# Top-k attention with two expert layers: all rests of the gate and value weights on GpSimd, and plain float32 scores on 64 array rows each

## The chip, the core and the metric

The kernel runs on one core of a Trainium2 chip. The engines named below are TensorE (PE: matrix products, with its weight loads shown apart as PEld), VectorE (DVE), ScalarE (ACT), GpSimd (POOL), and SyncE (SP), whose queue issues nearly all the transfers (DMA). The metric is the device time of one execution in microseconds (us). Three runs of the kernel before gave 1229.64, 1230.01 and 1234.19 us, so the median is 1230.01 us.

## The reference

Three stages in a row, all in float32:

```
scores = (q @ k.T) / sqrt(64)            # 4 batches, 8 heads, 576 tokens, head size 64
keep the 32 largest scores of each row, softmax over them, attn @ v
x   = heads side by side                  # 2304 tokens x 512
x   = (silu(x @ w_gate) * (x @ w_val)) @ w_out      # 512 -> 1536 -> 512
h   = x @ w_in;  out = (h * cos(h)) @ w_out2        # 512 -> 2048 -> 512
```

Which 32 scores are kept must agree with the reference, so the scores need nearly full float32 precision.

## The kernel before, in words

**The stages.** The 18 tiles of 128 tokens are handled in ten chunks of 1, 1, 2, 2, ... tiles. A unit is one tile and one head: there are 144 of them. For each unit PE computes a 128 x 576 score tile into the two PSUM banks of `sc`, ACT copies it to SBUF (L679), DVE finds the 32 largest values with four MAX8 and three MATCH_REPLACE8 (L706, L709), POOL makes two bounds of them (L720, L724), ACT masks and exponentiates (L737, L748), PE turns the result (L770) and multiplies it by V (L823, L826). When the four head pairs of a chunk are done, its tokens go through the gate and value product (L1072 for the first two chunks, L981 for the others) and the output product of the first expert layer (L1146). The second expert layer follows from about 760 us on.

**Two ways to multiply.** A plain float32 product goes through PE as two passes per matmul in the trace (64 score matmuls of L661 are 128 records). From the third chunk on, the gate and value weights are used as a pair instead: a rounded part (type fp32r, one pass) and a rest, the float32 weight minus its rounded part. `w1_rest` makes the pair for each of 24 half blocks of weights, number `i`: ACT makes the rounded part (`hi`, L295), then a subtraction makes the rest (L299), on VectorE for odd `i` and on GpSimd for even `i`. A pair is written over the slot of the raw half block before it, so number `i` waits for number `i - 1`. All of this has to be there before the gate and value product of the third chunk.

**Plain scores.** The first three chunks (32 units) and the 64 query rows of tile 4 that lie in batch 0 (`edge_score`, for all 8 heads) use plain float32 scores. Both heads of a pair lie in one K tile `KR[p]`, head 0 on partitions 0 to 63 and head 1 on 64 to 127, 576 columns wide. The queries of one head fill 64 partitions and the other 64 are set to zero (memsets of L454 and L537), so each matmul runs over all 128 array rows with 288 columns and the other head adds nothing.

**What sets the order.** The program is written by a planner (`Plan`): every step is a generator that yields an engine, an estimated cost, a function and a due time. The planner keeps a clock for each engine and always takes the ready step with the earliest due time. So a changed cost or engine reorders the instructions of the whole program. At run time every engine works through its own list strictly in that order. Rings (`Ring`) gate the use of buffers: five score tiles, one PSUM score tile, two buffers for output weights (`wo`), one for raw K or Q (`raw`). Because SP is also a list in order, a transfer that waits for a buffer holds back those written behind it.

**The output weights.** `wo0_proc` converts 12 blocks (ACT, then POOL at L249) while the first chunk uses them and stores them; the second chunk loads each of them again (L376, "wo<-wo"), two buffers at a time.

Of the kernel before, what the change touches and what calls it, by code (L numbers as in the profile page):

```python
# [9 lines left out]
F32 = mybir.dt.float32  # L10
# [11 lines left out]
B, H, S, D = 4, 8, 576, 64  # L22
# [8 lines left out]
CH = 256  # L31
# [5 lines left out]
FIRST = [sum(SIZES[:c]) for c in range(NCH)]  # L37
# [11 lines left out]
HALF = S // 2  # L49
# [7 lines left out]
RAWC = 3  # L57
SC_LEAD = 14.0
# [107 lines left out]
def topk_attention_moe_moe(ctx: ExitStack, tc: tile.TileContext, qT, kT, vP, w1, wo1, w2, out):  # L166
    nc = tc.nc
# [27 lines left out]
    att = opened("att", side="right")  # L195
# [5 lines left out]
    sc = psR.tile([128, 2, 512], F32, name="sc")  # L201
# [75 lines left out]
    def w1_rest(i, raw, due):  # L277
        f, a = divmod(i, 2)
        t = yield from convert(raw, due, r_top[i % 2], i // 2, tops[i % 2], True)
        x = raw.bitcast(F32)[:, :DM]  # L280
        W1X[f, a] = x.rearrange("p (g k f) -> p g k f", g=2, k=2)
        r_pre.free(i, t, plan)
        if i == 2 * NF1 - 1:
            r_k.free(0, t, plan)
        ev_w1x[f].set(t, plan)
        yield ev_gemm[PLAIN - 1, f]
        if i:
            yield ev_w1s[i - 1]
        due = W1S_FIRST + W1S_STEP * i
        st = {}  # L290

        def hi():
            st["w"] = w = wpool.tile([128, 2, DM], F32R, tag=slot(i), name=f"w1_{f}")
            W1[f, a] = w.rearrange("p s (g k f) -> p s g k f", g=2, k=2)
            nc.scalar.activation(w[:, 0], x, AF.Copy)  # L295

        yield "ACT", 0.52, hi, due, True
        eng, name, cost = (nc.vector, "DVE", 0.75) if i % 2 else (nc.gpsimd, "POOL", 1.25)
        t = yield name, cost, lambda: eng.tensor_sub(st["w"][:, 1], x, st["w"][:, 0]), due, True  # L299
        ev_w1s[i].set(t, plan)  # L300
        ev_w1[f].set(t, plan)
# [93 lines left out]
    K, Q, V = {}, {}, {}  # L395
# [18 lines left out]
    r_k, r_v = Ring(NK), Ring(NV)  # L414
# [16 lines left out]
    KR, QR = {}, {}  # L431
# [10 lines left out]
    EDGE = S % 128  # L442
    TE = S // 128
# [4 lines left out]
    edge = {}  # L448

    def edge_proc():  # L450

        def clear():
            edge["q"] = att.tile([128, NP, 2, EDGE], F32, tag="K", name="qe", bufs=r_k.n)
            nc.vector.memset(edge["q"], 0.0)  # L454

        yield "DVE", 0.5, clear, -1.0, True

        def load():
            for h in range(2):
                rows = slice(64 * h, 64 * h + 64)  # L460
                nc.sync.dma_start(edge["q"][rows, :, h],
                                  qT[:, rows, TE * 128:TE * 128 + EDGE].rearrange("p d n -> d p n"))

        t = yield "DMA", 1.0, load, 2.0, True
        for p in range(NP):
            for h in range(2):
                plan.start(edge_score(p, h), t)

    def edge_score(p, h):
        n = 2 * p + h  # L470
        due = EDGE_DUE + n
        yield ev_kr[p]
        yield r_edge[h].gate(p)
        ps = gvt if h == 0 else yt

        def qk():
            for s in range(2):
                nc.tensor.matmul(ps[s][64 * h:64 * h + EDGE, :HALF], edge["q"][:, p, h],
                                 KR[p][:, s * HALF:s * HALF + HALF])

        t = yield "PE", 1.25, qk, due, True
# [30 lines left out]
    def k_raw_proc(p):  # L512

        def load():
            KR[p] = att.tile([128, S], F32, tag="K", name="kr", bufs=r_k.n)
            for h in range(0 if p else 2):
                nc.sync.dma_start(KR[p][64 * h:64 * h + 64], kT[0, p, 64 * h:64 * h + 64])
            if p:
                nc.sync.dma_start(KR[p], kT[0, p])

        t = yield "DMA", 1.3, load, due_unit(2 * p) - 40.0, True
        ev_kr[p].set(t, plan)

    def q_raw_proc(c, p):
        n = SIZES[c] * 128
        yield r_q.gate(q_index(c, p))

        def load():
            QR[c, p] = att.tile([128, 2, CH], F32, tag="q", name="qr", bufs=r_q.n)[:, :, :n]
            queue = nc.scalar if c == 0 and p == 0 else nc.sync  # L530
            for h in range(2):
                rows = slice(64 * h, 64 * h + 64)
                queue.dma_start(QR[c, p][rows, h], qT[p, rows, FIRST[c] * 128:FIRST[c] * 128 + n])

        def clear():
            for h in range(2):
                (nc.vector if c == 0 and p == 0 else nc.gpsimd).memset(QR[c, p][64 - 64 * h:128 - 64 * h, h], 0.0)  # L537

        due = due_unit(unit_of[c, p, 0, 0]) - 30.0
        if c == 0 and p == 0:  # L540
            load()
            clear()
            t = 3.2
        else:
            t = yield "DMA", 1.3, load, due, True
            t = yield "POOL", 0.5 if n == CH else 0.3, clear, due, True
        ev_qr[c, p].set(t, plan)

    def k_proc(i, b, p, h):
# [89 lines left out]
    def unit_proc(u):  # L639
        c, p, t, h = units[u]  # L640
        segs = segments(FIRST[c] + t)
        due = due_unit(u)
# [14 lines left out]

        def qk():
            if c < RAWC:
                for s in range(2):  # L660
                    nc.tensor.matmul(sc[:, s, :HALF], QR[c, p][:, h, t * 128:t * 128 + 128],  # L661
                                     KR[p][:, s * HALF:s * HALF + HALF])
                return
            for b, r0, r1 in segs[::-1]:
                if not b:
                    continue
                k = K[b, p, h]
                for s in range(2):
# [10 lines left out]
                nc.scalar.activation(st["s"], sc[:, :, :HALF], AF.Copy)  # L679

        yield r_sc.gate(u)
        end = yield "PE", 0.575 * len(cuts) if c >= RAWC else 0.98, qk, due - SC_LEAD, True
# [1176 lines left out]
```

## Time and profile before

| | |
|---|---|
| median of three runs | 1230.01 us |
| the profiled execution, its own time | 1227.0 us |
| span of its trace | 1225.1 us |
| PE busy in the span | 1174.1 us (96%), 7720 matmul records |
| DVE busy | 1001.4 us (82%) |
| ACT busy | 937.6 us (77%) |
| POOL busy | 564.1 us (46%), all of it before 800 us |
| chain that ended last | PE 66%, DVE 8%, ACT 8%, DMA 8%, POOL 5% of the span |

The profiled execution is 3.0 us faster than the median and 1.9 us longer than its span. A share of busy time is an average over stages with different limits: DVE is close to full until about 760 us, POOL has nothing to do after 800 us, and PE is close to full from 200 us to the end. So the stage in which an instruction lies decides what it is worth.

### The profile page before, as it was taken

What the parts mean: (1) busy time and instruction counts of PE and PEld (TensorE: products, weight loads), DVE (VectorE), ACT (ScalarE), POOL (GpSimd) and SP (SyncE); (2) the same over time, 40 slices, a digit from 0 to 9 for tenths busy, and PEclk for the clock granted to TensorE, in tenths of its full rate; (3) what the DMA queues carried; (4) which work ended last, traced back from release to release, by engine and by line L of the source; (5) the groups of instructions that cost most, each with busy time, mean ns of one, the idle gap of its engine ahead of it and who ended that gap; (6) DMA issues with size and microseconds to landing.
All of it is one profiled execution on the core that took longest, in us unless ns stands there. A gap on an engine that the chain in (4) does not pass through costs nothing.

```text
span 1225.1 us, 23258 instructions
## 1 busy us (share of the span) xinstructions
PE 1174.1 (96%) x7720; PEld 1018.1 (83%) x7720; DVE 1001.4 (82%) x1985; ACT 937.6 (77%) x2093; POOL 564.1 (46%) x1028
## 2 busy tenths in 40 slices
PE   6799978998999999999999999999999999999998
PEld 3477746897988898988988888889999998888886
DVE  7999999999999999998999997267877778644541
ACT  4979989988999889887898887345856678755651
POOL 4888875876787776876776765300000000000000
PEclk9899999999999999999999999999999999999999
DMA  8555457664556655666655533464344276443430
GB/s 261 181 180 160 142 152 223 202 213 154 181 177 193 200 185 175 185 180 186 193 175 166 165 98 104 152 201 132 134 158 143 104 249 202 146 120 104 129 104 26
DMA packets 139464, 200.08 MB, mean 163 GB/s; under 512 B 19792, under 2 KB 88912, under 8 KB 139344
## 3 DMA queue, kind: packets, MB, share of 16 engines
q1 hardware_dynamic: 139184, 198.54, 51.6%
q8 instruction: 61, 1.00, 0.3%
q14 instruction: 59, 0.48, 0.1%
q10 hardware_dynamic: 160, 0.07, 0.0%
HBM read 151.23 MB, written 47.32 MB: 162 GB/s over the span
## 4 chain that ended last, share of the span: by engine, by line
PE 66%; DVE 8%; ACT 8%; DMA 8%; POOL 5%; issue 3%; SPq 1%; POOLq 0%; ACTq 0%; DVEq 0%
PE b L1758 16%; PE b L1481 13%; PE gv L981 12%; PE y L1146 9%; DVE m L706 4%; DVE w L709 3%; PE tp L770 3%; PE av L826 3%; DMA wo<-wo 3%; PE sc L670 3%; PE gvl L981 2%; DMA y<-yo 2%; DMA qx<-in_qT 2%; PE gv L1072 1%; ACT e L748 1%
## 5 line engine op out<-in xcount | busy, mean ns | idle before, releaser
L706 DVE MAX8 m<-w 128x8 f32<-128x576 f32 x432 | 309.6, 748 | 1.6
L981 PE MATMUL gv<-x,w 128*128 128x256 f32 x2016 | 283.7, 288 | 1.6 <-ACT hg L948 1.6
L981 PEld LDWEIGHTS gv<-x,w 128*128 128x128 f32 x2016 | 258.5, 190 | 8.9 <-ACT hg L948 3.0
L709 DVE MATCH_REPLACE8 w<-m,w 128x576 f32<-128x576 f32 x288 | 213.0, 742 | 0.0
L1758 PE MATMUL b<-w2o,gp 128*128 128x512 f32 x864 | 202.1, 396 | 0.0
L1758 PEld LDWEIGHTS b<-w2o,gp 128*128 128x128 f32 x864 | 162.2, 188 | 39.0
L1481 PE MATMUL b<-xc,w 128*128 128x288 f32 x1344 | 182.1, 297 | 0.1
L1481 PEld LDWEIGHTS b<-xc,w 128*128 128x128 f32 x1344 | 180.0, 188 | 1.0 <-ACT s L1568 0.4
L1146 PE MATMUL y<-wo,gh 128*128 128x512 f32 x400 | 149.4, 415 | 7.1 <-DMA wo<-wo 4.9
L706 DVE MAX8 m<-s 128x8 f32<-128x576 f32 x144 | 107.3, 745 | 15.2 <-ACT s L679 12.9
L748 ACT ACTIVATE e<-e,b 128x576 f32<-128x576 f32 x144 | 114.9, 798 | 4.6 <-POOL b L724 1.7
L737 ACT ACTIVATE e<-s,b 128x576 f32<-128x576 f32 x144 | 114.4, 795 | 2.5 <-POOL b L720 2.3
L770 PE MATMUL tp<-ident,e 128*128 128x128 f32 x648 | 97.8, 274 | 9.5 <-ACT pt L776 7.5
L709 DVE MATCH_REPLACE8 w<-m,s 128x576 f32<-128x576 f32 x144 | 106.9, 742 | 0.0
L776 ACT ACTIVATE pt<-tp 128x512 f32<-128x512 f32 (+1 forms) x216 | 102.1, 507 | 5.5 <-PE tp L770 4.2
L679 ACT ACTIVATE s<-sc 128x576 f32<-128x576 f32 x136 | 91.0, 669 | 18.4 <-PE sc L661 15.5
L1146 PEld LDWEIGHTS y<-wo,gh 128*128 128x128 f32 x400 | 74.9, 189 | 29.3 <-issue 4.9
L770 PEld LDWEIGHTS tp<-ident,e 128*128 128x128 f32 x648 | 77.0, 140 | 20.7 <-ACT pt L776 12.0
L670 PE MATMUL sc<-K,q 128*128 128x288 f32 x480 | 86.0, 304 | 1.7 <-ACT s L679 1.1
L1146 PE MATMUL y<-wo,gl 128*128 128x512 f32 x208 | 84.7, 414 | 2.1 <-POOL wo L249 0.8
L1044 POOL TENSOR_TENSOR gl<-vv,gh 128x256 fp32r<-128x256 f32 x84 | 62.4, 743 | 38.5 <-ACT gh L1040 27.6
L826 PE MATMUL av<-pt,V 128*64 128x256 f32 (+3 forms) x832 | 75.1, 323 | 0.0
(123 smaller groups left out, 2100.8 us busy)
## 6 DMA issues: line engine op xcount, KB each, us to landing
wo<-wo SPq DMA_DIRECT2D x96, 512.0 KB, 3.8
gr<-gd SPq DMA_DIRECT2D x72, 256.0 KB, 3.2
w_raw<-in_w SPq DMA_DIRECT2D x32, 511.8 KB, 4.4
V<-in_vP SPq DMA_DIRECT2D x52, 256.0 KB, 3.1
w<-in_w SPq DMA_DIRECT2D x24, 511.5 KB, 6.1
wo<-wo SPq DMA_DIRECT2D x36, 256.0 KB, 3.0
gd<-h SPq DMA_DIRECT2D x32, 288.0 KB, 2.4
gd<-r SPq DMA_DIRECT2D x32, 288.0 KB, 2.2
```

Source lines behind the costliest of these rows:

```text
L670: nc.tensor.matmul(sc[:r1, s, :HALF], q[:, a, (t - t0) * 128:(t - t0) * 128 + r1], k[:, s * HALF:s * HALF + HALF], start=a == 0, stop=a == 1)
L706: nc.vector.max(out=st["m"][:, 8 * i:8 * i + 8], in_=st["w"] if i else st["s"])
L709: nc.vector.match_replace(out=st["w"], in_to_replace=st["m"][:, 8 * i:8 * i + 8], in_values=st["w"] if i else st["s"], imm_value=LOWEST)
L737: nc.scalar.activation(st["e"], st["s"], AF.Prelu, bias=st["b"][:, 1:2], scale=SCALE, alpha=STEEP)
L748: nc.scalar.activation(st["e"], st["e"], AF.Exp, bias=st["b"][:, 2:3], scale=1.0, accum_out=smT[c, p, g][:, j:j + 1])
L770: nc.tensor.transpose(st["ps"][:, j - j0], e[:, j * 128:j * 128 + 128], ident)
L776: nc.scalar.activation(pt[:, j0:j1], st["ps"][:, :j1 - j0], AF.Copy)
L826: nc.tensor.matmul(av[64 * h:64 * h + 64, r0:r1], m[:, j, h], pt[:, 5 * h + j, r0:r1], start=False, stop=j == 3)
L981: nc.tensor.matmul(gv[g], W1[f, kk // 2][:, a, g, kk % 2], m, start=kk == 0 and i == 0, stop=kk == KT - 1 and i == 2)
L1146: nc.tensor.matmul(bank, m, w, start=f == 0 and n == 0, stop=f == NF1 - 1 and n == len(terms) - 1)
L1481: nc.tensor.matmul(ps[b], w[:, a, side, kk], x[:, e, kk], start=start and kk == 0 and m == 0, stop=kk == 1 and m == 2, skip_group_check=True)
L1758: nc.tensor.matmul(st["o"], g[:, a, cs], W2O[f][:, b], start=f == 0 and i == 0, stop=f == NF2 - 1 and i == 2)
```

## The change

There are two edits, and the planner then writes the whole program anew.

First, the rests of all 24 half blocks are made by GpSimd. Second, the plain scores use 64 array rows each. The K tile now holds both heads on the same 64 partitions, the first 288 columns of both heads on partitions 0 to 63 and the last 288 columns on 64 to 127; the queries lie twice, once on each half. A score tile is then four matmuls of 144 columns in place of two of 288, alternating between the upper and lower 64 array rows, and the two halves write different PSUM banks. The zero halves of the queries, and with them the memsets, go. K is loaded in pieces of 288 columns in place of 576, with twice as many transfers, and the queries are read twice. The planner's costs for these steps change too, 0.98 to 0.8 for a unit and 1.25 to 0.8 for an edge score.

```
-        eng, name, cost = (nc.vector, "DVE", 0.75) if i % 2 else (nc.gpsimd, "POOL", 1.25)
+        eng, name, cost = nc.gpsimd, "POOL", 1.25
...
-            nc.vector.memset(edge["q"], 0.0)
...
         def qk():
-            for s in range(2):
-                nc.tensor.matmul(ps[s][64 * h:64 * h + EDGE, :HALF], edge["q"][:, p, h],
-                                 KR[p][:, s * HALF:s * HALF + HALF])
+            for j in range(0, HALF, HALF // 2):
+                for s in range(2):
+                    rows = slice(64 * s, 64 * s + 64)
+                    nc.tensor.matmul(ps[s][64 * h:64 * h + EDGE, j:j + HALF // 2], edge["q"][rows, p, h],
+                                     KR[p][rows, h, j:j + HALF // 2])
...
-            for h in range(0 if p else 2):
-                nc.sync.dma_start(KR[p][64 * h:64 * h + 64], kT[0, p, 64 * h:64 * h + 64])
-            if p:
-                nc.sync.dma_start(KR[p], kT[0, p])
+            for heads in (slice(0, 2),) if p else (slice(0, 1), slice(1, 2)):
+                for s in range(2):
+                    nc.sync.dma_start(KR[p][64 * s:64 * s + 64, heads], kT[0, p, :, s * HALF:s * HALF + HALF]
+                                      .rearrange("(h d) n -> d h n", h=2)[:, heads])
...
-        def clear():
-            for h in range(2):
-                (nc.vector if c == 0 and p == 0 else nc.gpsimd).memset(QR[c, p][64 - 64 * h:128 - 64 * h, h], 0.0)
...
             if c < RAWC:
-                for s in range(2):
-                    nc.tensor.matmul(sc[:, s, :HALF], QR[c, p][:, h, t * 128:t * 128 + 128],
-                                     KR[p][:, s * HALF:s * HALF + HALF])
+                for j in range(0, HALF, HALF // 2):
+                    for s in range(2):
+                        rows = slice(64 * s, 64 * s + 64)
+                        nc.tensor.matmul(sc[:, s, j:j + HALF // 2], QR[c, p][rows, h, t * 128:t * 128 + 128],
+                                         KR[p][rows, h, j:j + HALF // 2])
```

How the order moves is shown at two places. The first is POOL's list where the last rests are made, around the K and Q rests of the fourth chunk. In the names, `w_10_...` and `w_11_...` are half blocks of weight blocks 10 and 11 (the last number is a buffer's), `K<-kx` and `q<-qx` are the rests of K and Q, `rs` and `x` belong to the normalised attention output, `b` to the bounds. Before:

```order
L569 TENSOR_TENSOR K<-kx,K 64x576
L299 TENSOR_TENSOR w_10_1916<-w_10_818,w_10_1916 128x512
L896 TENSOR_TENSOR rs<-rx,rs 128x256
L720 TENSOR_TENSOR b_1944<-m,cst 128x2
L724 TENSOR_TENSOR b_1944<-b_1944 128x1
L907 TENSOR_TENSOR x<-rs,x 128x256
L596 TENSOR_TENSOR q<-qx,q 128x256
L299 TENSOR_TENSOR w_11_1974<-w_11_870,w_11_1974 128x512
L596 TENSOR_TENSOR q<-qx,q 128x256
```

POOL's list at the same place after the change (line numbers above 450 are smaller by three to five):

```order
L564 TENSOR_TENSOR K<-kx,K 64x576
L299 TENSOR_TENSOR w_10_2019<-w_10_911,w_10_2019 128x512
L717 TENSOR_TENSOR b_2046<-m,cst 128x2
L721 TENSOR_TENSOR b_2046<-b_2046 128x1
L299 TENSOR_TENSOR w_11_2051<-w_11_934,w_11_2051 128x512
L852 TENSOR_SCALAR sm<-sm 128x4
L591 TENSOR_TENSOR q<-qx,q 128x256
L299 TENSOR_TENSOR w_11_2082<-w_11_963,w_11_2082 128x512
L591 TENSOR_TENSOR q<-qx,q 128x256
```

Between the K rest and the second Q rest there are now three weight rests where there were two, one of them directly ahead of the first Q rest.

The second place is PE's list while the gate and value product of the second chunk runs (`gv<-w,xw`). Before, a score unit is one row of two matmuls over 128 array rows:

```order
L1072 MATMUL gv_100<-w_5_436,xw_115 128x256 x2
L1072 MATMUL gv_100<-w_5_480,xw_116 128x256 x2
L661 MATMUL sc<-kr,qr 128x288 x2
L1146 MATMUL y_102<-wo,gl_1117 128x512
L770 MATMUL tp<-ident,e 128x128 x8
```

After, in PE's list in the same product:

```order
L1069 MATMUL gv_100<-w_1_192,xw_115 128x256 x2
L1143 MATMUL y_102<-wo,xw_117 128x512
L1069 MATMUL gv_100<-w_1_219,xw_116 128x256 x2
L658 MATMUL sc<-kr,qr 128x144 x4
L1069 MATMUL gv_101<-w_2_245,xw_115 128x256
```

A score unit still stands between the products of the expert layer, as four matmuls of 144 columns, and the list changes between whole-array and half-array matmuls at each of them.

## Rows read from the trace of the kernel before

**Rows 1.** Stretches: width, busy us (instructions) of PE, PEld, DVE, ACT, POOL; clock, DMA, GB/s

```profile
10.00:60.00 50.00, 37.96 (x174) 22.45 (x173) 46.94 (x103) 40.06 (x86) 35.43 (x64) 0.94 0.68 222
...
92.00:116.00 24.00, 21.71 (x144) 16.79 (x144) 23.71 (x52) 22.04 (x56) 19.05 (x41) 1.00 0.45 139
116.00:140.00 24.00, 23.84 (x119) 17.82 (x118) 24.00 (x48) 23.87 (x54) 20.44 (x31) 1.00 0.50 155
140.00:165.00 25.00, 22.98 (x112) 15.70 (x111) 25.00 (x52) 24.58 (x57) 22.90 (x32) 1.00 0.52 171
165.00:200.00 35.00, 27.04 (x130) 15.45 (x127) 30.91 (x64) 29.38 (x63) 19.29 (x31) 0.95 0.60 173
200.00:760.00 560.00, 547.41 (x4151) 491.77 (x4151) 542.18 (x1120) 491.04 (x1194) 402.78 (x749) 1.00 0.57 176
```

**Rows 2.** Instructions of line 299 (duration ns min/median/max)

```profile
L299 DVE TENSOR_TENSOR w<-w,w x12: 667/693/1710, 119.1 to 187.7; 128x512 fp32r<-128x512 f32 x12
```

**Rows 3.** Chain that ended last, in order of time, start (start us, us, what)

```profile
4.77 2.27 PE sc L661 x4
...
7.77 2.30 PE sc L661 x4
...
10.78 0.75 DVE m L706
```

**Rows 4.** The same chain, from 125 to 160 us

```profile
125.52 0.97 PE sc L661 x4
...
130.17 1.88 PE av L826 x16
132.05 1.92 PE gv L1072 x8
...
136.68 1.73 PE gv L1072 x8
...
157.04 1.17 PE sc L661 x4
...
159.07 0.89 PE tp L770 x8
```

**Rows 5.** The same chain, from 160 to 200 us

```profile
163.10 0.84 DVE w L299
...
178.24 1.42 POOL K L569
...
184.99 1.28 POOL w L299
...
188.20 3.10 DMA wo<-wo
```

**Rows 6.** Groups by line (busy us, mean ns of one, idle before)

```profile
L896 POOL TENSOR_TENSOR rs<-rx,rs 128x256 f32<-128x256 f32 x32 | 24.4, 762 | 17.5 <-ACT rx L837 17.2
...
L299 POOL TENSOR_TENSOR w<-w,w 128x512 fp32r<-128x512 f32 x12 | 15.4, 1280 | 4.2 <-ACT w L295 4.0
...
L299 DVE TENSOR_TENSOR w<-w,w 128x512 fp32r<-128x512 f32 x12 | 10.1, 843 | 1.9 <-ACT w L295 1.9
...
L537 POOL MEMSET qr<- 64x128 f32 (+1 forms) x22 | 5.2, 237 | 1.2
```

**Rows 7.** Line 299 alone, 116 to 165 us: DVE busy (instructions), POOL busy (instructions)

```profile
116.00:165.00 49.00, 7.38 (x8) 10.25 (x8) 1.00 0.51 163
```

**Rows 8.** POOL and DVE in order of time, 156 to 165 us

```profile
157.64 0.74 POOL L596 TENSOR_TENSOR q<-qx,q 128x256 fp32r<-128x256 f32 x1
...
157.80 1.13 DVE L299 TENSOR_TENSOR w<-w,w 128x512 fp32r<-128x512 f32 x1
...
158.32 1.21 POOL L896 TENSOR_TENSOR rs<-rx,rs 128x256 f32<-128x256 f32 x1
```

**Rows 9.** SP's transfers in order of time, start of the program

```profile
0.72 1.20 SPq L517 DMA_DIRECT2D kr<-in_kT  x2
...
6.45 1.91 SPq L272 DMA_DIRECT2D w<-in_w  x3
```

More of the change, by code (lines that the diff above doesn't have):

```diff
@@ L453, in clear @@
             edge["q"] = att.tile([128, NP, 2, EDGE], F32, tag="K", name="qe", bufs=r_k.n)
-            nc.vector.memset(edge["q"], 0.0)
-        yield "DVE", 0.5, clear, -1.0, True
+        yield "-", 0.0, clear, -1.0, True
         def load():
-            for h in range(2):
-                rows = slice(64 * h, 64 * h + 64)
-                nc.sync.dma_start(edge["q"][rows, :, h],
-                                  qT[:, rows, TE * 128:TE * 128 + EDGE].rearrange("p d n -> d p n"))
+            for s in range(2):
+                for h in range(2):
+                    nc.sync.dma_start(edge["q"][64 * s:64 * s + 64, :, h],
+                                      qT[:, 64 * h:64 * h + 64, TE * 128:TE * 128 + EDGE].rearrange("p d n -> d p n"))
         t = yield "DMA", 1.0, load, 2.0, True
@@ L476, in qk @@
         def qk():
-            for s in range(2):
-                nc.tensor.matmul(ps[s][64 * h:64 * h + EDGE, :HALF], edge["q"][:, p, h],
-                                 KR[p][:, s * HALF:s * HALF + HALF])
-        t = yield "PE", 1.25, qk, due, True
+            for j in range(0, HALF, HALF // 2):
[3 more added lines that the diff above has]
+                                     KR[p][rows, h, j:j + HALF // 2])
+        t = yield "PE", 0.8, qk, due, True
         if n == 2 * NP - 1:
@@ L514, in load @@
         def load():
-            KR[p] = att.tile([128, S], F32, tag="K", name="kr", bufs=r_k.n)
-            for h in range(0 if p else 2):
-                nc.sync.dma_start(KR[p][64 * h:64 * h + 64], kT[0, p, 64 * h:64 * h + 64])
-            if p:
-                nc.sync.dma_start(KR[p], kT[0, p])
+            KR[p] = att.tile([128, S], F32, tag="K", name="kr", bufs=r_k.n).rearrange("p (h n) -> p h n", h=2)
+            for heads in (slice(0, 2),) if p else (slice(0, 1), slice(1, 2)):
+                for s in range(2):
+                    nc.sync.dma_start(KR[p][64 * s:64 * s + 64, heads], kT[0, p, :, s * HALF:s * HALF + HALF]
+                                      .rearrange("(h d) n -> d h n", h=2)[:, heads])
         t = yield "DMA", 1.3, load, due_unit(2 * p) - 40.0, True
@@ L530, in load @@
             queue = nc.scalar if c == 0 and p == 0 else nc.sync
-            for h in range(2):
-                rows = slice(64 * h, 64 * h + 64)
-                queue.dma_start(QR[c, p][rows, h], qT[p, rows, FIRST[c] * 128:FIRST[c] * 128 + n])
-        def clear():
-            for h in range(2):
-                (nc.vector if c == 0 and p == 0 else nc.gpsimd).memset(QR[c, p][64 - 64 * h:128 - 64 * h, h], 0.0)
+            for s in range(2):
+                queue.dma_start(QR[c, p][64 * s:64 * s + 64], qT[p, :, FIRST[c] * 128:FIRST[c] * 128 + n]
+                                .rearrange("(h d) n -> d h n", h=2))
         due = due_unit(unit_of[c, p, 0, 0]) - 30.0
@@ L541, in q_raw_proc @@
             load()
-            clear()
             t = 3.2
@@ L545, in q_raw_proc @@
             t = yield "DMA", 1.3, load, due, True
-            t = yield "POOL", 0.5 if n == CH else 0.3, clear, due, True
         ev_qr[c, p].set(t, plan)
@@ L659, in qk @@
             if c < RAWC:
-                for s in range(2):
-                    nc.tensor.matmul(sc[:, s, :HALF], QR[c, p][:, h, t * 128:t * 128 + 128],
-                                     KR[p][:, s * HALF:s * HALF + HALF])
+                for j in range(0, HALF, HALF // 2):
+                    for s in range(2):
+                        rows = slice(64 * s, 64 * s + 64)
+                        nc.tensor.matmul(sc[:, s, j:j + HALF // 2], QR[c, p][rows, h, t * 128:t * 128 + 128],
+                                         KR[p][rows, h, j:j + HALF // 2])
                 return
@@ L681, in unit_proc @@
         yield r_sc.gate(u)
-        end = yield "PE", 0.575 * len(cuts) if c >= RAWC else 0.98, qk, due - SC_LEAD, True
+        end = yield "PE", 0.575 * len(cuts) if c >= RAWC else 0.8, qk, due - SC_LEAD, True
         if h and (c, t) == (RAWC - 1, SIZES[c] - 1):
```

## The prediction

> **What bounds the kernel now.** I read the busy time by stretch first, then the chain that ended last in order of time, then the groups by line, and last DVE and POOL side by side where they meet.
>
> The stretches show which stage can give anything [rows 1]. From 200 to 760 us PE is busy 547.41 of 560 us. Neither edit touches an instruction there: the last weight rest on DVE begins at 187.7 us [rows 2], and the plain scores are over by then. So the change can only move the moment at which PE's long unbroken list begins. What is won before 200 us is kept to the end, since DVE, with 542.18 of 560 us, also has some room; what is only freed on DVE, and does not bring PE's work forward, is worth nothing.
>
> Before 200 us the bound changes three times. At first it is DVE's top-k, after a start on transfers and PE: two score tiles at 4.77 and 7.77 us, each over 2.2 us long, and then a long stretch on DVE, whose third instruction at 10.78 us has to wait for the second tile [rows 3]. From 125.52 to 160 us all 38 pieces of the chain are PE's, with no wait between them; six of them are plain scores, five of 0.97 us and one of 1.17 us [rows 4]. From 160 to 200 us the chain hops between latencies: a weight rest on DVE, K and weight rests on POOL, and the loads of the output weights, over 3 us each, written on SP's list behind the loads of K and Q [rows 5].
>
> The trap is DVE's row. It is busy 24.00 of 24 and 25.00 of 25 us from 116 to 165 us [rows 1], so taking work from it looks like pure gain. But PE has 46.8 and ACT 48.5 of those 49 us as well, and the chain goes through PE. Three lists are full at once; emptying one of them shortens nothing by itself.
>
> **The change part by part.**
>
> *The weight rests.* Removed are twelve subtractions on DVE, 10.1 us busy, mean 843 ns; added are twelve on POOL at 1280 ns, 15.4 us [rows 6]. What hides the time that DVE gets back is PE's unbroken stretch and the loads after it; only the piece of 0.84 us at 163.10 us stands on the chain [rows 5]. I count -0.8 us; the bounds are 0 and, without the cover, all -10.1 us (a rival below).
>
> On POOL most of the added time falls between 116 and 188 us. There the rest waits in line with the K and Q rests, and SP's list holds the next K load, and the output weights written behind it, until the Q rest frees the one raw buffer. Of the chain from 178.24 to 188.20 us one weight rest is a piece today (1.28 us at 184.99 us) [rows 5]; in the new list three stand between the K rest and the second Q rest where two stood. I count one more, +1.3 us. The bounds are 0, when it falls into one of POOL's gaps (19.29 of 35 us busy [rows 1]), and +5.1 us, when the four that lay on DVE after 165 us [rows 7] all fall on that chain, 4 x 1.28.
>
> One thing comes back to POOL. When a rest on DVE begins during a POOL instruction it lasts until that has ended, and the next POOL instruction is drawn out: the rest at 157.80 us takes 1.13 us against a median of 693 ns, and the POOL product at 158.32 us takes 1.21 us against a mean of 762 ns [rows 2, 6, 8]. That is some 0.45 us for each meeting; I count one for every second rest. The Trainium skill says the same in its "GPSIMD Engine Reference", section "Specifications": GpSimd's SBUF interfaces are shared with VectorE, with contention against instructions of VectorE that have two SBUF inputs. The trace agrees for pairs that overlap. Taken at its word for all eight rests that lie on DVE from 116 to 165 us, the rule would give POOL back 8 x 0.45 = 3.6 us there.
>
> *The scores.* A unit goes from four passes of 288 columns to eight of 144 on half the rows, so twice as many weight loads. If the halves do not overlap it stays at 0.97 us. The nearest row for overlap is the attention product, which alternates between two column halves of the array: 16 passes of 256 columns in 1.88 us, 0.118 us each, against 8 passes of 256 columns over the whole array in 1.73 us, 0.216 us each [rows 4]. That is a share of 0.54, and would make 0.53 us of the 0.97. The nearest row for a load of 128 columns at each short matmul is the transposes, 8 in 0.89 us, 0.11 us each [rows 4]; eight loads at that rate are 0.89 us. Neither is nearer than the other, the first being like it in the halves and the second in the loads, so I take the middle, 0.70 us: 0.27 us less. For the six scores on the chain this is 6 x 0.27 = -1.6 us, between 0 and 6 x 0.44 = -2.6 us. The other plain scores and the eight edge scores lie beside DVE or ACT and count nothing.
>
> The Trainium skill has a rule against this: its page "TensorEngine Tiling (Array Packing)", section "Tiling Modes", says that changing the tiling mode, not just the tile, drains the engine, and the new list changes it at every score. In the trace the change from column halves back to the whole array leaves no gap (130.17 + 1.88 = 132.05 us), and 16 passes at half of 0.216 us are 1.73 us of the 1.88 [rows 4]. So at most 0.15 us per change is seen; by the rule the six scores would lose up to 0.9 us of their gain.
>
> *The start.* PE is slow there, 2.27 and 2.30 us per score [rows 3]. The same share, 0.70 of 0.97, takes 0.63 us from each; the second tile is then 1.26 us earlier, and DVE, which starts 0.63 us earlier and wins back its wait, follows. I count -1.2 us, between 0 and -1.7 us. Against it, five more transfers at about 0.6 us each (1.20 us for two) stand on SP's list ahead of the first raw weights, which move from 6.45 to about 9.4 us [rows 9]. POOL, which converts them, has 14.6 us idle from 10 to 60 us [rows 1], and this hides it; without that cover it would be +2.9 us.
>
> *The memsets.* The 22 on POOL are 5.2 us [rows 6], with the gaps named to hide them: 0. Those on DVE end before its first tile arrives: 0. The additional reads of Q lie beside other transfers: 0.
>
> The sum is -1.2 - 1.6 - 0.8 + 1.3 = -2.3 us. The profiled execution took 1227.0 us, so 1224.7 us; the median of the runs is 1230.0 us, 3.0 us above it, and on that scale the forecast is 1227.7 us.
>
> **The rivals.**
>
> *DVE's time counts in full.* PE's stretch from 125 us is unbroken perhaps only because DVE hands it units at that pace, and with DVE 10.1 us lighter everything slides forward. For it: DVE is at 100% from 116 to 165 us. Against it: ACT has only 2.5 us idle in the 73 us from 92 to 165 us (70.49 busy) and 5.6 us from there to 200 us [rows 1], and its work for these units is unchanged. Those 8.1 us and the start's 1.2 us are a ceiling below DVE's own gain, and give the time: -9.3 us, 1220.7 us.
>
> *The halves do not overlap.* Then start and scores give 0, what remains is -0.8 + 1.3 = +0.5 us, and with six changes of mode at 0.15 us +1.4 us: 1230.5 to 1231.4 us. For it speaks that no row shows row halves side by side; against it the column halves do run so.
>
> *POOL becomes the bound* (the other side). From 116 to 165 us POOL is busy 20.44 + 22.90 = 43.3 of 49 us [rows 1]. Eight of the twelve rests lay on DVE there [rows 7]: +8 x 1.28 = 10.2 us, less four meetings at 0.45 us, 1.8 us, makes 51.7 us in 49. That overflows by 2.7 us, and the chain after 165 us takes its 5.1 us: +7.8 us, less the start's 1.2 us, is +6.6 us, 1236.6 us. It decides from the point at which POOL's list has no gap between the conversions of the output weights and PE's output product waits for them. For it: an engine in order that is full delays bounds and K rests behind weight rests that nobody needs yet. Against it: the stretch after 165 us has 15.7 us of gaps.
>
> **How the numbers follow.** My forecast gets 0.33, no overlap 0.15, DVE in full 0.33, POOL 0.19. A measurement of this kernel can tell about 0.5%, 6.15 us, from no change; the forecast and no overlap lie within it. So faster 0.33, same 0.48, slower 0.19. The forecast's own range is 1225 to 1232.5 us: all gains at their bounds without POOL's cost (-5.1 us), and half of POOL's bound without gains (+2.6 us). As cases of both signs matter, the whole range reaches from 1218 us (DVE in full, and the scores at 0.53 us, which takes ACT no time but PE another 1 us and the start 0.5 us) to 1236.5 us, with about 1 in 10 left out on each side.
>
> **What would show it.** In the profile of the changed kernel: DVE's third instruction near 9.5 us; a score unit near 0.70 us on the chain, not 0.97; no rest on DVE, and DVE no longer full from 116 to 165 us but waiting for ACT's copies of scores; POOL near 50 of 49 us there; ACT still full; a weight rest on POOL on the chain more often than once between 160 and 200 us. I am wrong if the third chunk's gate and value product starts more than 6 us sooner or later than it does now, or if PE's idle time between 200 and 760 us, 12.6 us now, changes by as much.

## The result, and the profile after

The changed kernel takes 1235.7 us (median of 12 runs, 1232.3 to 1237.4) against 1228.4 us of the kernel before beside it. The ratio is 1.0059 with a 95% interval of 1.0045 to 1.0073: slower by some 7 us, where 2.3 us less were forecast. The profiled execution took 1233.53 us, its span is 1231.7 us (before: 1225.1).

The stretches of the changed kernel, to be read against [rows 1]: width, busy us (instructions) of PE, PEld, DVE, ACT, POOL; clock, DMA share, GB/s.

```profile
10.00:60.00 50.00, 35.99 (x252) 25.92 (x253) 46.57 (x100) 40.05 (x87) 34.88 (x58) 0.85 0.87 264
...
92.00:116.00 24.00, 22.91 (x150) 15.81 (x151) 24.00 (x51) 23.64 (x57) 17.10 (x35) 1.00 0.47 147
116.00:140.00 24.00, 24.00 (x146) 17.11 (x145) 23.97 (x53) 24.00 (x56) 23.25 (x37) 1.00 0.47 156
140.00:165.00 25.00, 19.63 (x105) 12.90 (x103) 23.09 (x47) 21.36 (x49) 23.04 (x30) 0.93 0.44 139
165.00:200.00 35.00, 25.98 (x128) 14.46 (x127) 24.89 (x52) 31.09 (x68) 23.73 (x37) 1.00 0.64 178
...
200.00:760.00 560.00, 543.51 (x4097) 485.61 (x4095) 540.84 (x1110) 486.08 (x1178) 399.43 (x740) 1.00 0.56 175
```

Four things are to be seen. POOL has more from 116 to 165 us, 46.3 of 49 us for 43.3. PE, which had 22.98 of 25 us from 140 to 165 us, now has 19.63. From 200 to 760 us, where neither edit changes an instruction, PE has lost 3.9 us. And from 10 to 60 us the mean granted clock is 0.85, where it was 0.94, although PE is busy there for 35.99 us and not 37.96.

The first two tiles of the program, on DVE in order of time (start us, us, engine, line, out<-in; idle time before). They answer to [rows 3].

```profile
6.21 0.76 DVE L703 MAX8 m<-s 128x8 f32<-128x576 f32 x1 [5.33 <-ACT s L676]
...
8.54 0.74 DVE L703 MAX8 m<-s 128x8 f32<-128x576 f32 x1
```

The second tile reaches DVE at 8.54 us, without a wait; before it was 10.78 us. The plain score at PE's two levels of clock (granted 0.50 from 60 to 64 us, 1.00 from 70 us), from the chain of waits, for the 0.97 us of [rows 4]. The last three pieces follow each other without a gap:

```profile
61.89 1.26 PE sc L658 x8
...
76.68 0.69 PE sc L658 x8
77.37 1.92 PE gv L1069 x8
79.30 0.69 PE sc L658 x8
```

The eight gate and value matmuls between two scores take 1.92 us. In the kernel before, eight such matmuls that stand between whole-array work take 1.73 us (136.68 us, [rows 4]). So a score in halves takes 0.69 us itself and some 0.19 us more from its neighbours, 0.88 us for 0.97.

The rests and the POOL product beside them, by line (busy us, mean ns | idle before), for [rows 6]:

```profile
L299 POOL TENSOR_TENSOR w<-w,w 128x512 fp32r<-128x512 f32 x24 | 30.6, 1276 | 4.0 <-ACT w L295 3.7
L893 POOL TENSOR_TENSOR rs<-rx,rs 128x256 f32<-128x256 f32 x32 | 23.6, 737 | 16.4 <-ACT rx L834 15.9
```

Where the chain before was PE's without a break from 125 to 160 us [rows 4], it now goes through ACT up to 147 us and then through POOL, until PE's output product (L1143) starts at 161.07 us:

```profile
142.06 0.53 ACT wo L247
...
147.55 1.29 POOL wo L249
...
152.03 1.28 POOL w L299
153.31 1.25 POOL wo L249
...
155.25 1.23 POOL w L299
...
159.78 1.25 POOL wo L249
161.03 0.04 issue
161.07 3.48 PE y L1143 x4
```

PE itself, in order of time, stands for 4.53 us before that product:

```profile
155.78 0.76 PE L658 MATMUL sc<-kr,qr 64*128 64x144 f32 x8
161.07 2.08 PE L1143 MATMUL y<-wo,gl 128*128 128x512 f32 x2 [4.53 <-POOL wo L249]
```

This looks like the rival "POOL becomes the bound" to the letter: weight rests between the conversions of the output weights, and PE waiting for the last of them. The experiments show that taking work off POOL does not give the time back, or gives back a part of it at most.

### The profile page after: what moved, and what is told of

Its sections match the earlier page's. It is cut to its first block, busy times and chain, and to the rows that moved or that the text cites. A ratio compares the mean times of both kernels' runs of the same rounds, so it can differ in the third digit from the quotient of the medians.

```text
span 1231.7 us, 23509 instructions
## 1 busy us (share of the span) xinstructions
PE 1172.6 (95%) x7880; PEld 1017.8 (83%) x7880; DVE 996.9 (81%) x1970; ACT 939.1 (76%) x2093; POOL 569.3 (46%) x1018
## 3 DMA queue, kind: packets, MB, share of 16 engines
q8 instruction: 62, 1.02, 0.3%
## 4 chain that ended last, share of the span: by engine, by line
PE 60%; ACT 11%; DVE 9%; DMA 8%; POOL 7%; issue 4%; SPq 1%; POOLq 0%; ACTq 0%; DVEq 0%
PE b L1755 16%; PE b L1478 13%; PE gv L978 10%; PE y L1143 7%; DVE m L703 4%; DVE w L706 4%; PE av L823 3%; PE tp L767 2%; PE sc L667 2%; DMA kx<-in_kT 2%; PE gvl L978 2%; ACT e L745 1%; DMA wo<-wo 1%; ACT e L734 1%; ACT pt L773 1%
## 5 line engine op out<-in xcount | busy, mean ns | idle before, releaser
L1143 PE MATMUL y<-wo,gh 128*128 128x512 f32 x400 | 147.9, 411 | 5.4 <-DMA wo<-wo 4.1
L767 PE MATMUL tp<-ident,e 128*128 128x128 f32 x648 | 100.6, 280 | 7.2 <-ACT pt L773 5.0
L1143 PEld LDWEIGHTS y<-wo,gh 128*128 128x128 f32 x400 | 74.7, 188 | 26.4 <-issue 5.1
L1143 PE MATMUL y<-wo,gl 128*128 128x512 f32 x208 | 86.2, 421 | 9.8 <-POOL wo L249 5.4
```

The source lines that it names most:

```text
L767: nc.tensor.transpose(st["ps"][:, j - j0], e[:, j * 128:j * 128 + 128], ident)
L1143: nc.tensor.matmul(bank, m, w, start=f == 0 and n == 0, stop=f == NF1 - 1 and n == len(terms) - 1)
```

## The experiments

All ratios are against the kernel before on the same chip (medians 1230.6 to 1233.3 us), 5 rounds each. Executions of one kernel scatter by some 4 to 7 us, once 9, to either side of its median, so a single trace shows places, and only the ratios show sizes. "Order" is the order of all lists as the planner writes it; it depends on the durations and engines that the program tells the planner, and these can be held while the work is changed. The traces show that this holds the lists: with equal neighbours joined, PE's list agrees in 1280 of 1284 places between the kernel before and both edits in the old order, and in 916 between the kernel before and the changed one.

**Both edits in the old order.** The work of the change; the planner is told the old engines and durations.

```
-        eng, name, cost = nc.gpsimd, "POOL", 1.25
+        eng = nc.gpsimd
+        name, cost = ("DVE", 0.75) if i % 2 else ("POOL", 1.25)
-  end = yield "PE", ... if c >= RAWC else 0.8, qk
+  end = yield "PE", ... if c >= RAWC else 0.98, qk     (edge scores 1.25, memsets 0.5 and 0.3: as before)
```

> Both edits are in, but the planner is given the engines and costs that it had before, so that every list keeps the order of the kernel before. Theory O (the loss comes from the new order, after 200 us, where neither edit touches an instruction): the loss goes, ratio to before 0.994 to 1.001, since what the edits win before 200 us stays. Theory P (the loss comes from GpSimd's added load before 200 us): slower as the changed kernel is, ratio 1.004 to 1.008. Theory S (the start and the doubled reads of Q cost it): also 1.004 to 1.008.

Measured: 1.0034 [1.0017, 1.0052]. It lies between the ranges of Theory O and of Theories P and S. With the order held, the work of the edits costs 0.34% where a gain of 0.19% was forecast; whether the changed kernel's 1.0059 is more than this, the two intervals alone do not tell.

**The old work in the new order**, the reverse of it.

> The counterpart: every instruction is that of the kernel before (rests on both engines, scores over 128 rows, memsets), but the planner is given the changed kernel's engines and costs, so that the lists stand in its order. Theory O: slower without any of the work having changed, ratio 1.004 to 1.010 (the changed kernel has 1.006). Theories P and S: like before, 0.998 to 1.002.

Measured: 1.0089 [1.0068, 1.0110]. An order alone can cost 0.9%, without one changed instruction. But in this trace most of the loss is made before 200 us, not after it as Theory O has it: the third chunk's product starts at 211.8 us, for 200.2 us in the kernel before, 11.6 of the 16.3 us between the two spans.

**Each edit alone, with the order that goes with it.**

> Only the rests are moved to GpSimd, with the planner's costs for it. Theory P: slower by all of the loss, ratio 1.004 to 1.010. Theory O: it has an order of its own, so its ratio is not the sum's share; anything from 0.995 to 1.008. Theory S: like before, 0.998 to 1.002.

> Only the scores on 64 array rows, with the planner's costs for them and rests on both engines. Theory P: as before or faster, 0.995 to 1.001. Theory S: slower by all of the loss, 1.004 to 1.008. Theory O: an order of its own, 0.995 to 1.008. Under all of them a score unit on PE's unbroken stretch takes 0.69 us, as in the changed kernel.

Measured: the rests 0.9964 [0.9948, 0.9980], the scores 1.0020 [1.0001, 1.0039]. The edit that loads POOL makes the kernel faster, and the two do not add up to 1.0059.

**Each edit's work alone, in the old order.**

```
rests:   eng = nc.gpsimd;  name, cost = ("DVE", 0.75) if i % 2 else ("POOL", 1.25)
scores:  the halves, their loads and no memsets; told 0.98, 1.25 and 0.5 as before
```

> The first edit's work alone: every rest of the gate and value weights is made by GpSimd, and all lists keep the order of the kernel before. Scores and memsets are as before. Known: the first edit with its own order is at 0.9964, both edits in the old order are at 1.0034. Theory A (GpSimd's added load costs where it stands in the way of the output weights' conversions, and the first edit's own order made up for it): 1.003 to 1.005, about 1235 us, and GpSimd over 47 of 49 us from 116 to 165 us. Theory B (taking the rests from VectorE is a gain by itself, and the loss of the two edits in the old order comes from the scores): 0.996 to 0.999, about 1227 us. Theory C (the load is nothing to the end, each order has its own time of some tenths of a per cent): within 0.999 to 1.001.

> The second edit's work alone: plain scores in halves of the rows, the additional reads of Q, no memsets; all lists keep the order of the kernel before, and half of the weight rests stay on VectorE. Theory A (GpSimd's load is what costs in the old order): 0.998 to 1.000, about 1228 us, the third chunk's gate and value product 1 to 3 us sooner than 200.2 us, from the start and six shorter scores. Theory B (the scores cost: more transfers ahead of the weights, and shorter work on TensorE at a low clock): 1.003 to 1.005, about 1235 us, the product later than 200.2 us or the clock lower from 30 to 70 us.

Measured: rests 1.0027 [1.0008, 1.0045], scores 0.9996 [0.9980, 1.0012]. So most of the 0.34% of both in the old order is the rests'. The trace has one new wait that could carry it, in the waits of ACT from 116 to 200 us (who <- releaser: us in total, times, longest):

```profile
ACT w L295 <- POOL w L300: 2.7, 5, 0.7
```

The rounded part of one weight (L295) is written into the buffer that the rest before it reads. The old order was written for a rest that takes 0.75 us on DVE; on POOL it takes 1.28 us and waits its turn, and ACT, which has no slack there up to 165 us [rows 1], stands five times. The changed kernel and the rests alone, whose orders know of the longer rest, have no such wait. That the loss comes from this wait is not shown: both edits in the order told 1.00 (below) have it too, 2.2 us in five times, and there they cost 0.12%, within the noise.

**Both edits in the first edit's order, and a nudge.** The second kernel has the work of before to the last instruction; only the number told for a plain score is 0.96 for 0.98.

> Both edits' work, in the order that the planner wrote for the first edit alone (the scores and memsets keep their old planned costs). Against the changed kernel only the order differs; against the first edit alone (0.9964) only the scores' work. Theory A or C (the changed kernel's loss lies in the order that the scores' new planned costs bring): 0.994 to 0.998, about 1225 us, as the first edit alone or up to 2.3 us below it. Theory B (the scores' work costs by itself): 1.001 to 1.004, about 1233 us.

> The kernel before, its work unchanged to the last instruction; only the planner is told that a plain score takes 0.96 us instead of 0.98, which rewrites the lists at about as many places as either edit does. Theory C (each order has its own time, and what the change brought is of that size): more than 0.2% off on either side, 0.990 to 0.998 or 1.002 to 1.010, with the third chunk's product more than 2 us from 200.2 us or its start-to-end time more than 2 us from 1024.9 us. Theories A and B (orders matter only where a changed piece of work meets them): 0.999 to 1.001, about 1229 us.

Measured: 0.9977 [0.9956, 0.9998] and 0.9995 [0.9980, 1.0011]. The same work as the changed kernel's, 0.8% faster by its order alone. The nudge gave nothing, against what Theory C expected of it.

**Half of the rests back on DVE, in the changed kernel's order.**

```
-        eng, name, cost = nc.gpsimd, "POOL", 1.25
+        eng, name, cost = nc.vector if i % 2 else nc.gpsimd, "POOL", 1.25
```

> The changed kernel, its order of every list kept; only every second weight rest is made by VectorE again, at the same place of the program, so that GpSimd has twelve rests (15.4 us) less. Theory P (in the changed kernel's order GpSimd's rests hold up the output weights' conversions and with them TensorE, 4.5 us at 154 us): that wait falls under 1.5 us, the third chunk's product starts 3 us or more sooner than 199.5 us, ratio 1.001 to 1.004. Theory O (the order is slower as such, whoever makes the rests): 1.005 to 1.009, and the wait may go without a gain at the end.

Measured: 1.0057 [1.0034, 1.0080], as the changed kernel. PE's wait for the conversion did not go; PE's waits from 100 to 205 us, and PE at the place:

```profile
PE y L1143 <- POOL wo L249: 6.6, 3, 5.0
```

```profile
164.39 2.07 PE L1143 MATMUL y<-wo,gl 128*128 128x512 f32 x2 [5.04 <-POOL wo L249]
```

What POOL waits for in this kernel from 116 to 165 us:

```profile
POOL wo L249 <- ACT wo L247: 2.3, 4, 0.9
```

POOL has time now (17.18 of 24 and 19.95 of 25 us) and waits for ACT's part of the same conversion, which stands at 161.81 us in ACT's list, behind copies of scores and of weights. So the wait and the gain that Theory P foresaw did not come, and the third chunk's product starts later, at 203.7 us. The exchange is not clean, though: on the way to that conversion a rest, now on VectorE (155.41 us, 1.45 us long), holds up ACT for 1.04 us. The next run takes work off GpSimd and gives it to nobody.

**The joining of the output weights left out.** In the changed kernel's order, 4 columns are copied instead of 512 added, twelve times; ACT's conversion before it writes float32 instead of integers. The edit is shown shortened.

```
-        t = yield "POOL", 1.27, lambda: nc.gpsimd.tensor_tensor(words[:, :DM], top, rest, op=OP.add), due, True
+            nc.gpsimd.tensor_copy(raw.bitcast(F32)[:, :4], raw.bitcast(F32)[:, 4:8])   # output weights only
```

> The changed kernel in its own order; left out is the joining of the twelve output weight tiles on GpSimd (4 columns are copied instead of 512 added, some 1.2 us less each, 14 us in all), so the output product has other weights. Theory W (the changed kernel's loss is TensorE's wait for these conversions at 147 to 161 us): that wait falls from 5.4 to under 2 us, the third chunk's product starts 2.5 us or more sooner than 199.5 us, and the ratio is 1.000 to 1.003. Theory D (what is lost is lost after 200 us, where the list has TensorE wait for ScalarE's and the queue's small pieces): the product starts sooner and the ratio stays at 1.004 to 1.007.

Measured: 1.0035 [1.0010, 1.0060]. Some 14 us less on POOL, and PE still waits, for the short copy behind ACT's conversion, which ends at 161.59 us (PE's waits from 100 to 205 us):

```profile
PE y L1149 <- POOL wo L251: 3.6, 1, 3.6
```

The third chunk's product starts at 200.6 us, not sooner than the changed kernel's 199.5 us. Theory W falls; whether the 0.24% between the two ratios is a gain stays open, since their intervals overlap. What is shown is that the wait, the one striking row of the changed kernel, falls only from 5.4 to 3.6 us when POOL's work is taken away, since ACT's conversion is late as well.

**The changed kernel's work, the planner told other numbers for a plain score.**

> The changed kernel's work; only the planner's number for a plain score is 0.70 us, what a score takes in the trace at the full clock, in place of 0.80 us. Theory T (the loss comes from a planned cost that is wrong): the truer number makes a better order, 0.996 to 1.002. Theory C (the lists come out otherwise at each nudge, and each has its own time): anywhere from 0.997 to 1.008, without regard to how true the number is.

> The changed kernel's work; only the planner's number for a plain score is again 0.98 us (of the memsets it knows that they are gone, of the edge scores it has the new number). Theory N (the lower number for the scores is what brought the slow order): 0.996 to 0.999, as both edits in the first edit's order (0.9977). Theory M (it is the memsets taken off its list or the edge scores' number): 1.004 to 1.007. Theory C: anywhere between.

> The changed kernel's work; the planner's number for a plain score is 0.72 us. The lists come out almost as with 0.70 us (24 lines of TensorE's list stand elsewhere, of some thousands). Theory C (the list decides) and theory T (the truer number decides) both expect what 0.70 gave: 0.993 to 0.998. If it is above 1.001, the gain of 0.70 was not the list's.

> The changed kernel's work; the planner's number for a plain score is 0.68 us, as near to the 0.69 us of the trace as 0.70, but the lists come out otherwise at hundreds of places. Theory T (a true number makes a good order): 0.993 to 0.998, as with 0.70. Theory C (each list has its own time, whatever the number): anywhere from 0.995 to 1.008, as likely above 1.000 as below.

Measured: told 0.70: 0.9957 [0.9934, 0.9979]; 0.98: 1.0038 [1.0018, 1.0057]; 0.72, nearly the same list as 0.70: 0.9976 [0.9957, 0.9995]; 0.68: 1.0033 [1.0015, 1.0051]. With 0.80 it is the changed kernel, 1.0059. The instructions are the same in all five. There is no trend in the number, and 0.68 is as true to the measured 0.69 us as 0.70: Theory T falls by the 0.68, Theory N by the 0.98, and Theory M, whose range the 0.98 nearly meets, by the 0.70 and 0.72, which have the same memsets and edge scores. C is what is left. It had said so little that hardly a result could have gone against it, and even so 0.70 came out just below its 0.997; what speaks for it is that intervals of the same work do not overlap. 0.72 agrees with 0.70 as nearly as their intervals tell.

What an order takes is seen best in PE's busy time up to 200 us, to 800 us and to the end: width, busy (instructions), clock, DMA share, GB/s. First the kernel before, then the changed kernel, then the same work told 0.70.

```profile
0.00:200.01 200.01, 168.06 (x838) 0.97 0.58 182
200.00:800.00 600.00, 585.67 (x4428) 1.00 0.56 173
800.00:1240.00 440.00, 420.41 (x2459) 1.00 0.43 136
```

```profile
0.00:200.01 200.01, 164.78 (x999) 0.94 0.62 188
200.00:800.00 600.00, 583.51 (x4394) 1.00 0.55 173
800.00:1240.00 440.00, 424.36 (x2492) 1.00 0.43 137
```

```profile
0.00:200.01 200.01, 164.85 (x1016) 0.96 0.62 190
200.00:800.00 600.00, 586.00 (x4426) 1.00 0.55 173
800.00:1240.00 440.00, 417.27 (x2441) 1.00 0.43 136
```

Take busy from width, and for the last row from the span's end (1225.1, 1231.7 and 1222.2 us). PE's idle time is 32.0 + 14.3 + 4.7 us before, 35.2 + 16.5 + 7.3 us in the changed kernel, 35.2 + 14.0 + 4.9 us told 0.70. The changed kernel has 8.1 us more idle than before and 1.5 us less busy, together the 6.6 us of the spans. Against the same work told 0.70 it loses no idle time before 200 us, 4.9 us after it, and 4.5 us more busy time; where the latter comes from with the same instructions is only partly seen (the clock up to 200 us is 0.94 for 0.96).

PE's waits from 200 to 790 us show that this is no single wait (first the kernel before, then the changed one):

```profile
PE gv L981 <- ACT hg L948: 1.6, 5, 0.5
...
PE y L1146 <- POOL gl L1044: 0.7, 2, 0.4
```

```profile
PE gv L978 <- ACT hg L945: 3.0, 7, 0.8
PE y L1143 <- POOL gl L1041: 2.2, 4, 1.0
```

**A second nudge of the kernel before**, told 1.00 for 0.98, its work unchanged.

> The kernel before, its work unchanged; the planner is told 1.00 us for a plain score instead of 0.98. Told 0.96 it gave 0.9995. Theory C: within 0.994 to 1.006 and most likely 0.2% or more from 1. Theory T (the old number is true at the full clock, 0.97 us, so a nudge harms little): 0.999 to 1.002.

Measured: 0.9955 [0.9937, 0.9972]. A number that is less true by 0.02 us gains 5.5 us. With 0.98 and 0.96 this makes three orders of the same work that span 0.45%.

**Each work in the other's best order.**

> Both edits' work, in the order that the planner wrote for the kernel before when told 1.00 us for a score (0.9955 with the work of before). Theory A (work and order add up): 0.9955 + 0.0034, so 0.997 to 1.001. Theory F (an order is good for the work it was planned for): 1.002 or more.

> The work of the kernel before, in the order that the planner wrote for the changed work when told 0.70 us for a score (0.9957 with both edits). Theory A (work and order add up): 0.9957 - 0.0034, so 0.990 to 0.995. Theory F: 0.998 or more; in the changed kernel's order the work of before lost 0.3% against both edits, which would give 0.9987 here.

Measured: 0.9967 [0.9951, 0.9983] and 1.0077 [1.0056, 1.0099]. The first is at the lower end of Theory A's range, the second agrees with Theory F. **The old work in the first edit's order:**

> The work of the kernel before, in the order that the planner wrote for the first edit alone; every second weight rest on VectorE. Known: the first edit with this order 0.9964, with the old order 1.0027. Theory O (this order is better as such): 0.993 to 0.997, TensorE's third chunk's product at 196 us or sooner. Theory F (an order is good for the work that it was planned for): 1.000 to 1.004, VectorE's list now having 10.1 us that the plan does not know of.

Measured: 0.9990 [0.9971, 1.0009], between the two theories.

All ratios by order (down) and work (across):

| Order written for | old work | rests | scores | both |
|---|---|---|---|---|
| before (score 0.98) | 1 | 1.0027 | 0.9996 | 1.0034 |
| before, told 0.96 | 0.9995 | | | |
| before, told 1.00 | 0.9955 | | | 0.9967 |
| rests alone | 0.9990 | 0.9964 | | 0.9977 |
| scores alone | | | 1.0020 | |
| the change (0.80) | 1.0089 | | 1.0057 | **1.0059** |
| the change, told 0.98 | | | | 1.0038 |
| the change, told 0.72 | | | | 0.9976 |
| the change, told 0.70 | 1.0077 | | | 0.9957 |
| the change, told 0.68 | | | | 1.0033 |

Read across, an edit's work moves the time by -0.3 to +0.3% in orders that were not written for the short scores; in two that were, the old, longer work loses 0.3 and 1.2% against the new. Read down the last column, the same work spans 1.0%. The versions told 0.70 and 1.00 and the rests alone beat the kernel before by 0.4%; which of them is best the intervals do not tell.

## Why the prediction was wrong

The step that failed is the first: "Neither edit touches an instruction there [...] So the change can only move the moment at which PE's long unbroken list begins", with "What is won before 200 us is kept to the end". The third chunk's product did start sooner, at 199.5 for 200.2 us, but from there to the end the profiled execution took 1032.2 us where it had taken 1024.9 us. Nor does an early start decide elsewhere: with the changed work told 0.98, the product starts at 191.8 us and the kernel is still at 1.0038. The edits change no instruction after 200 us; they change the numbers that the planner writes all lists from, and the sum had no term for that. The orders tried for this work give it a size: 0.9957 to 1.0059, some 12 us, five times the forecast gain. A second part failed beside it: the gain of the work itself. Held in the three orders that were not written for the short scores, both edits gave +0.34, +0.12 and -0.13%, for the -0.19% of the sum, so even in the best of them no gain clear of noise was measured.

The terms, one by one:

- **The start**, -1.2 us: the two scores take 2.00 and 1.33 us for 2.26 and 2.29, together 1.2 us less, as put, though not 0.63 us each. The second tile is 2.2 us sooner because the first product also starts 1.3 us earlier (3.50 for 4.77 us), which the sum did not have. (What the prediction calls DVE's third instruction is the fourth of the top-k.) The raw weights moved to 9.78 us (9.4 expected), and no load of them is on the chain at the start.
- **The score**, 0.70 us: measured 0.69 us. The number was the middle of two bounds, neither of them nearer, so that it hit is in part luck. The term missed what a change between whole-array and half-array matmuls takes from the instructions beside it: 0.19 us per score among gate and value matmuls (above), 0.15 us with an output product ahead (1.12 us for 1.02) and transposes behind (1.09 us for 1.04). The prediction's own rows had it: behind the column halves, eight gate and value matmuls take 1.92 us at 132.05 us, against 1.73 us at 136.68 us [rows 4], and only the missing gap was read. The Trainium skill's rule in "TensorEngine Tiling (Array Packing)", section "Tiling Modes", is that a change of mode drains the engine. The trace agrees with it: the doubt that the prediction priced at up to 0.9 us for six scores, and left out of the sum, came true, at 0.9 to 1.1 us.
- **Six scores on PE's stretch**, -1.6 us: at 0.84 to 0.88 us each, six of them save 0.5 to 0.8 us. The last gate and value product of the second chunk does start at 148.3 for 154.4 us, but the order differs too, so how much of this is the scores' is not shown. Then PE stands from 156.5 us for output weights that ACT and POOL have not converted, and what was won is lost. The prediction named this trap for DVE ("Three lists are full at once") and did not apply it to PE.
- **Rests off DVE**, -0.8 us, **and on POOL's chain**, +1.3 us: together +0.5 us in the sum. In the old order they cost 0.27%, 3.3 us; the longer rest holds up ACT's next copy there, 2.7 us in all, on an engine for which the sum had no term; that this carries the loss is not shown (above). In the changed order one piece of a rest is on the chain between 165 and 200 us (0.75 us), not more than one.
- **The meetings of DVE and POOL**, 1.8 us for POOL from 116 to 165 us, a meeting for every second rest: under-counted. In the trace of the kernel before, eight of the twelve rests on DVE draw out a POOL instruction, by 0.35 to 0.47 us each and 3.4 us in all; six of the eight from 116 to 165 us do, 2.6 us. With all rests on POOL no other instruction of POOL is drawn out so from 116 to 200 us. Five of them are not the product that the prediction read (now L893, mean 762 to 737 ns, 0.8 us over its 32) but the bounds (now L717 and L721, mean 199 to 192 and 208 to 197 ns, 2.6 us over 144 each). A rest that meets a longer POOL instruction does not end with it, as the prediction reads, but some 0.55 us later: the one at 157.80 us ends at 158.93 us, and the instruction that it met at 158.38 us. The Trainium skill's "GPSIMD Engine Reference", section "Specifications", names this contention, and the trace agrees.
- **The rival "POOL becomes the bound"** gave 1236.6 us, close to the 1235.7 us measured, and its picture was in the trace. That the number was so near is luck, for the mechanism does not carry the loss: with twelve rests taken off POOL in the same order the time stays (1.0057), with 14 us of other work taken off it the ratio is still 1.0035, and with the rests alone and their own order POOL is fuller (23.50 + 24.32 of 49 us) and the kernel faster (0.9964). A part of the loss in this order may still be POOL's.
- **What was to show me wrong** did not: the third chunk's product moved by 0.7 us and PE's idle time from 200 to 760 us from 12.6 to 16.5 us, both less than the 6 us that I had set. A bound of 6 us on each part lets a loss of 7 us pass that is spread over several. Of the other signs, ACT did not stay full from 116 to 165 us (45.4 of 49 us, for 48.5), and POOL came to 46.3 us there, not 50. Two bounds of the prediction do not follow from its rows, and neither moves the forecast: the start with scores at 0.53 us is some 2.1 us, not 1.7, and DVE in full with such scores some 1219 us, not 1218.

What stays open: which feature of an order makes it slow, and what the rests' 0.3% in the old order come from. The losses are small waits in many places, and no single one was shown to carry them.

## What to carry to other kernels

Where a planner writes the lists from told durations, an edit is two changes: its work, and a new order of everything. Hold the order while changing the work, and the work while changing the order, before giving either a cause; and nudge one number of the kernel before to learn how far orders scatter, for an edit smaller than that scatter can't be judged by one build. A striking wait in the new trace is not the loss until its removal has moved the end. And a change without a gap in the chain is not free: compare what its neighbours take with the same instructions elsewhere.

## What was not expected of the hardware

Less work on PE at the start went with a lower clock there. From 10 to 60 us the eight kernels with whole-row scores have a mean granted clock of 0.93 to 0.97, the twelve with half-row scores 0.83 to 0.93, a mix of the two levels, 2.4 and 1.2 GHz, on which the unit takes 0.69 or 1.26 us (above). The row tells nothing of the very start: it reads 1.00 up to 34 us in both kernels, though up to 22 us the scores take 2.26 us before and 1.33 us or more after the change, much as they do later at the lower level (2.15 and 1.33 us). From 30 to 65 us the means are 0.85 to 0.95 and 0.71 to 0.85. In the old order, rests alone and then scores alone:

```profile
10.00:60.00 50.00, 38.62 (x173) 23.29 (x173) 46.97 (x102) 39.24 (x86) 35.63 (x65) 0.93 0.67 220
```

```profile
10.00:60.00 50.00, 36.24 (x274) 26.61 (x276) 49.23 (x107) 42.97 (x93) 37.14 (x62) 0.89 0.86 269
```

So part of the time that the halves save is given back by the clock, and the transfers rise from 0.67 to 0.86 of the DMA engines with the doubled reads of Q and the split loads of K. DVE is nearly full there, 49.23 of 50 us, and in the old order the sum of all this is nothing (0.9996). That DVE hides it is not shown: the chain of the changed kernel goes through PE at the low clock at 61.89 us (above).

Half-row scores in float32, the two halves of the array's rows side by side, take 0.69 of 0.97 us with twice the weight loads, not half; with what each change to and from whole-array matmuls takes from its neighbours they cost 0.84 to 0.88 us.
